# VectorE instead of TensorE turns u over from tile 6 on, and the state products join the scores-values step

## The chip, the core and the metric

The kernel runs on one core of a Trainium2 chip. The core has TensorE (matmuls, PE in the profile, with its weight loads as PEld), VectorE (DVE), ScalarE (ACT), GpSimd (POOL) and SyncE (SP, which issues every DMA of this kernel). Each engine works through its own queue in order; semaphores tie the queues together. TensorE writes only into PSUM, GpSimd here touches only SBUF. The metric is the device time of one execution in microseconds.

## What is computed

An attention layer with a recurrent state (batch 4, 8 heads, 768 steps, head size 40), then two dense layers on its 3072 tokens:

```
C = f_stab * C + i_stab * outer(v_t, k_t);  n = f_stab * n + i_stab * k_t
y_t = sigmoid(o_t) * (C q_t) / max(|n q_t|, 1)

h = x @ w_in                      # 320 -> 1024
solu = h * softmax(h)
ln = (solu - mean) / sqrt(var + 1e-6) * g_ln
x2 = ln @ w_out                   # 1024 -> 320

out = max(x2 @ w1, x2 @ w2, x2 @ w3) @ w_out2     # 320 -> 768 -> 320
```

## The kernel before

The recurrence is cut into chunks of 128 steps; a tile t is one chunk of one batch entry, 24 tiles (NT) in all, six (NC) to a batch entry. Within a chunk attention is a product of scores and values, and the state C passes from chunk to chunk. The 128 steps of a tile are also the 128 tokens that the dense layers take. Products in full precision are made of several matmuls on a high part (cast to fp32r) and the remainder; `split` (lines 299 to 303) makes both: a cast on ScalarE, then a subtraction on VectorE or GpSimd.

Each tile has several processes, generators that issue a few instructions and yield. The ORDER string, written out by a planner, is the order in which they are stepped, and so the order of every engine's queue and of the DMA queue: `A7*3` means three steps of process A of tile 7, and `~n` puts n dummy matmuls ahead. The processes that matter here:

- Q (`att_qk`, line 330) loads q and k; from tile 6 (NF) on it splits them into `qkh` and `qkl`, stores both to DRAM and loads them back stacked on 120 partitions. W makes the decay matrix, V loads values and weighted keys `kw`.
- S (`att_scores`, line 418) makes scores `ps` and multiplies them with the decay into `Pr`. I (`att_inter`, line 430) makes the part of the carried state, `pi`, from tile 6 on.
- Y (`att_out`, line 495) multiplies `Pr` with V into `py` (line 501), for tiles 1 to 5 adds C times q in the same PSUM group (line 504), adds `pi`'s part, and stores the result.
- T (`att_state`, line 457) makes the state products `pc` (line 472), adds them to the decayed C, and from C of tile 6 on splits it into `cst`, with two copies by DMA.
- X (`tokens`, line 530) loads the result with partitions as features, gates it and splits it into `xh` and `xl`.
- A (`layer1`, line 551): `ph` (two products into one PSUM tile with one buffer), its maximum (line 568), `e` = exp (line 571), `u` = ph * e (line 576), centred into `e` (line 580 on ScalarE or 582 on VectorE), squares summed (line 584), then `e` turned over in eight 128x128 blocks by TensorE into `pu` (line 592), four blocks to a PSUM tile, split in two halves into `uh` and `ul` (line 604), multiplied with w_out into `px` (line 613), scaled into `x2`, turned into `pq`, split into `x2h` and `x2l`. `e` and `u` have one buffer each; `ul` takes that of `e`, `uh` that of `u`.
- U (`layer2`, line 634) makes nine products `pe` per pair of tiles, in two PSUM buffers; P (line 652) takes the maximum of three and splits it into `h`; F (line 669) multiplies with the last weight into `po` and stores the output.

Three lists at the top say which of these operations run where: CENTER (the centring on ScalarE), POOL (the remainder of a split on GpSimd, and some products of X), VECTOR (the others on VectorE, GpSimd if not named; `P3` there is the remainder of `h`). PSUM tiles with tag "r" share four buffers.

## Time and profile before

| | us |
|---|---|
| median of 3 runs | 610.88 |
| lowest and highest | 607.91, 611.41 |
| the profiled execution | 608.91 |
| its span, first to last instruction | 607.1 |
| TensorE busy in it | 583.9 |
| VectorE busy | 380.0 |
| ScalarE busy | 345.0 |
| GpSimd busy | 198.6 |

Mean granted clock of TensorE: 0.975 of full speed. Busy times are of one profiled execution; matmuls overlap each other, so for what one costs TensorE the start of the next instruction is read, not the duration. "Idle before, releaser" in a row is the time that an engine waited and what ended it.

### The profile page before, as it was taken

Reading aid. Unit: us, or ns where it says so; the run is one execution under the profiler, and the core shown is the slowest. Engines: PE = TensorE matmul, PEld = TensorE weight load, DVE = VectorE, ACT = ScalarE, POOL = GpSimd, SP = SyncE. Lnnn points to the kernel's source line nnn. Section 1 sums busy time; section 2 is a strip of 40 time slices with the busy share of each in tenths; the row PEclk is TensorE's granted clock in tenths of the full one; section 3 lists DMA queues with packets and bytes.
Section 4 is the critical chain, followed back from the end, with each engine's and each line's share of the span. In section 5 each row is a group of like instructions: output and inputs, shape, how many; then the busy total and the mean of one; then the engine's idle time right before and its main releaser. Section 6 shows DMA issues by size and latency. Waiting matters only on the chain.

```text
span 607.1 us, 12327 instructions
## 1 busy us (share of the span) xinstructions
PE 583.9 (96%) x4688; PEld 542.7 (89%) x4688; DVE 380.0 (63%) x620; ACT 345.0 (57%) x671; POOL 198.6 (33%) x238
## 2 busy tenths in 40 slices
...
GB/s 301 335 201 269 262 203 213 259 230 179 162 148 169 159 64 118 231 217 206 156 107 183 185 180 204 195 173 181 144 207 219 85 40 19 37 5 11 12 32 25
DMA packets 56841, 95.97 MB, mean 158 GB/s; under 512 B 13926, under 2 KB 36510, under 8 KB 56782
## 3 DMA queue, kind: packets, MB, share of 16 engines
...
q14 instruction: 22, 0.18, 0.1%
...
## 4 chain that ended last, share of the span: by engine, by line
PE 74%; DVE 7%; DMA 7%; issue 4%; ACT 3%; SPq 2%; POOL 2%; DVEq 0%; ACTq 0%; POOLq 0%
PE pe L648 30%; PE px L613 12%; PE ph L566 11%; PE po L679 9%; PE pu L592 3%; PE py L501 3%; PE ps L423 3%; DMA nq<-rn 2%; PE pi L452 1%; PE pq L625 1%; POOL stA L269 1%; DMA qst<-qks 1%; PE pc L472 1%; DMA nd<-y 1%; DVE ul L302 1%
## 5 line engine op out<-in xcount | busy, mean ns | idle before, releaser
L648 PE MATMUL pe<-x2h,w 128*128 128x256 f32 x1080 | 166.8, 285 | 0.0
L648 PEld LDWEIGHTS pe<-x2h,w 128*128 128x128 f32 x1080 | 143.9, 189 | 2.0 <-issue 0.8
L648 PE MATMUL pe<-x2l,w 128*128 128x256 f32 x648 | 112.3, 282 | 0.0
L648 PEld LDWEIGHTS pe<-x2l,w 128*128 128x128 f32 x648 | 92.2, 188 | 0.0
L662 DVE TENSOR_TENSOR tmp<-pe,tmp 128x512 f32<-128x512 f32 x72 | 49.4, 686 | 55.9 <-PE pe L648 47.3
L679 PE MATMUL po<-w,h 128*128 128x320 f32 x432 | 67.6, 311 | 0.0
L566 PE MATMUL ph<-w,xh 128*128 128x512 f32 x240 | 65.9, 404 | 0.8 <-ACT xh L300 0.8
L613 PE MATMUL px<-w,uh 128*128 128x320 f32 x384 | 65.4, 313 | 0.4 <-DVE ul L302 0.4
L679 PEld LDWEIGHTS po<-w,h 128*128 128x128 f32 x432 | 63.7, 188 | 0.3 <-issue 0.2
L396 ACT ACTIVATE Wm<-Wm,aT 128x128 f32<-128x128 f32 x184 | 57.9, 393 | 6.4 <-POOL Wm L367 6.3
L613 PEld LDWEIGHTS px<-w,uh 128*128 128x128 f32 x384 | 58.8, 190 | 1.4 <-DVE ul L302 0.6
L566 PEld LDWEIGHTS ph<-w,xh 128*128 128x128 f32 x240 | 42.8, 191 | 8.5 <-ACT xh L300 1.1
L300 ACT CAST h<-tmp 128x512 fp32r<-128x512 f32 x36 | 22.2, 618 | 44.9 <-DVE tmp L662 44.9
L269 POOL TENSOR_TENSOR stA<-stA,raw 128x640 int32<-128x640 int32 x20 | 37.3, 1885 | 31.8 <-DVE raw L264 8.6
L367 POOL TENSOR_SCALAR_AFFINE_SELECT Wm<-Wm 128x1024 f32<-128x1024 f32 x24 | 28.9, 1205 | 54.3 <-DMA Wm<-rows_m 54.3
L576 DVE SCALAR_TENSOR_TENSOR u<-ph,e 128x1024 f32<-128x1024 f32 x24 | 29.2, 1216 | 26.0 <-ACT e L571 25.9
L426 DVE TENSOR_TENSOR Pr<-ps,Wm 128x512 f32<-128x512 f32 x48 | 32.2, 684 | 18.1 <-PE ps L423 11.2
L501 PE MATMUL py<-Pr,V 128*42 128x128 f32 x384 | 31.1, 290 | 12.8 <-DVE Pr L426 12.8
L571 ACT ACTIVATE e<-ph,st 128x1024 f32<-128x1024 f32 x24 | 26.8, 1117 | 25.8 <-PE px L613 18.9
L302 DVE TENSOR_TENSOR ul<-pu,uh 128x512 fp32r<-128x512 f32 x48 | 32.3, 685 | 14.3 <-ACT uh L300 7.8
L566 PE MATMUL ph<-w,xl 128*128 128x512 f32 x144 | 40.9, 392 | 0.0
L616 ACT ACTIVATE x<-px,st 128x320 f32<-128x320 f32 x24 | 12.6, 525 | 45.8 <-PE px L613 45.6
...
## 6 DMA issues: line engine op xcount, KB each, us to landing
...
```

Source lines behind the costliest of these rows:

```text
L269: pt(out=i32(A[:, j]), in0=i32(A[:, j]), in1=i32(low[:, j]), op=ALU.add)
L302: sub(out=lo, in0=x, in1=f(hi), op=ALU.subtract)
L367: nc.gpsimd.affine_select(out=W, in_=W, pattern=[[0, H], [1, P]], compare_op=ALU.is_ge, fill=-NEG, base=0, channel_multiplier=-1)
L396: nc.scalar.activation(out=W[:, h], in_=W[:, h], func=AF.Exp, scale=-1.0, bias=aT[:, c, b * H + h:b * H + h + 1])
L426: tt(out=Pr, in0=ps, in1=at[t, "W"][:, hh * 4:hh * 4 + 4], op=ALU.mult)
L501: mm(py[half(hh, VW), i], lhsT=at[t, "V"][:, hh * 4 + i], rhs=at[t, "P", hh][:, i], start=True, stop=(qg is None))
L566: mm(out_n, lhsT=a, rhs=x, start=(i == 0), stop=(i == len(passes) - 1))
L576: nc.vector.scalar_tensor_tensor(out=u, in0=ph, scalar=-2.0 ** -15, in1=e, op0=ALU.mult, op1=ALU.mult, accum_out=s(3))
L613: mm(px, lhsT=a, rhs=x, start=(i == 0), stop=(i == len(passes) - 1))
L648: mm(pe[:, j], lhsT=a, rhs=x, start=(i == 0), stop=(i == len(passes) - 1))
L662: tt(out=tmp, in0=pe, in1=tmp, op=ALU.max)
L679: mm(po[o], lhsT=h2[:, a, m, o * P:o * P + P], rhs=made[f"last{m // 2}"][:, x * WC + m % 2 * DM:][:, 0:DM], start=(m0 == 0 and i == 0), st ...
```

## The change

From tile 6 (NV) on, process A turns `e` over with VectorE: 16 instructions, each of eight 32x32 blocks (32 partitions x 256 elements), four to a step, from `e` into a new SBUF tile `eT`. The split of u is then one cast of 128x1024 and one subtraction of the same size, the latter on GpSimd for the tiles that POOL names with `u`. The transposes on TensorE and their PSUM tiles go for these tiles.

`state_products` is `pc`'s part of T as a function; from tile 6 (NJ) on, Y calls it right behind its own matmuls, in the same step. In Y all V products now come ahead of the products with C, and only the first matmul of a PSUM half starts it and only the last stops it. `qkl` is written over the raw tile. ORDER is the same up to the middle of its tenth line, but for one step of Q8 that comes later, and new from there, and the three lists are new: among others P0 to P9 leave VECTOR, all Q leave POOL. Of ORDER the lines around tiles 12 to 16 and 21 stand here.

```diff
--- before.py
+++ after.py
@@ -15,9 +15,9 @@
 AX = mybir.AxisListType
 ET = mybir.EngineType
 
-CENTER = "A0v A11v A14v A17v A18v A1v A21v A23v A2v A3v A4v A5v A6v A7v A8v"
-POOL = "D16 D19 Q10 Q11 Q19 Q20 Q21 Q22 Q23 Q7 X10s X12m X13s X14m X14s X16m X17m X18s X19s X1s X20m X20s X21m X21s X23m X23s X4m X4s X5m X5s X7m X7s X8m X8s"
-VECTOR = "I1 I2 I3 I4 I5 P0 P1 P11 P3 P4 P5 P7 P8 P9 T1 T10 T2 T3 T4 T7 V0 V1 V12 V13 V15 V18 V19 V2 V20 V4 V7 V9 X0g X11g X15g X17g X19g X21g X22g X23g X2g X3g X5g X6g"
+CENTER = "A0v A10v A11v A12v A13v A14v A15v A16v A19v A1v A20v A22v A23v A3v A4v A6v A8v A9v"
+POOL = "A11u A13u A14u A16u A21u A6u A7u D16 X0m X10m X10s X11s X13m X13s X14m X14s X16s X17s X20m X20s X21m X21s X22s X23m X2m X4m X4s X5m X6s X7m X7s X8s X9m X9s"
+VECTOR = "I1 I2 I3 I4 I5 P10 P11 T1 T10 T13 T16 T19 T22 V0 V1 V13 V15 V16 V18 V3 V4 V7 X0g X13g X14g X16g X17g X18g X1g X20g X3g X5g X6g"
 
 B, H, S, D = 4, 8, 768, 40
 P = 128
@@ -30,6 +30,8 @@
 K1 = FF1 // P
 K2 = FF2 // P
 NF = 6
+NV = 6
+NJ = 6
 NB = 1
 NA = 24
 VW = D + 2
...
+V16 X13 W15 A12 A11 A12 S15.0 X13*2 T14*2 T15 A11 I15 Q16 Q17 A12*2 Y14 P4 T14 S15.1 X13 U4 S15.0 U4 S15.1 Y14*2 P4
+A12 P4*3 W17 Y15 T15 U4 V16 A13 V18 W16 A12 P4 A12*2 W16 A11*2 A12 X14 Q17 I15*4 A12*3 A13 Y14 Q16 Q17 T15*2 P4*2 F4*3
+Y15 W17 U5*2 Y14 X14*2 S16.1 A12*2 T15*2 W16 S16.1 I16 S16.0*2 W18 X14 A12 A13*2 F4 X14*2 T16 A13 A12 P5 Y15 Q17 P5
+A13*2 I16 A14 W17 F4 I16*2 O5 A13*2 Q18 W17 Q18 F4 U5 P5 A14 A13 Y16 A13*2 U5 Y15 T16*2 Y15 Y16 Q17 P5 U5 P5 I16 V17
+P5 Y15 A13 Y16 A12 T16 Q18 P5 Y16 A14 U5 P5 Y16 A13*2 P5 O5 A14*2 U5 I17 P5 S17.1 S17.0 Q18 T16 P5 A13 S17.0 U5 A12
+S17.1 X15*3 T16 P5 A12 Y16 I17 X15 W18 A14 I17*2 U5 W18 X15*2 A13*2 P5 Y17 P5 Y17 Q19*3 P5 A15 Q18 X16*2 F3 A14 A13 F5
+I17 Y17 A14*2 Q19 F5 S18.0*2 A14*2 F5*2 X16 U6 Q20 A14*2 X16 P6 A15 V18 X16 Y17 X17 W19 V20 A14 S18.1 V20 W18 S18.1 U6
+A15 A14*2 Y17 Y18 A15 P6 Q19 T18 A14 U6 A15 W20 T18*2 X16 Q20 A15 U6 Y18 Y17 A16*2 Q20 T18 W19 T18 P6 F5 A15*2 S19.0
+A15*2 Y18 Q20 W19 P6 A14 A15*2 S19.0 A14 S19.1 A15*2 W19 S19.1 X17*2 I19*2 P6*2 X17 A16 U6 A15 Q21 U6 V19 Y18 I19*2
...
+A20*2 P8 U8 P8 U8 A18 A19 Y22 X21 S23.1 A20 P8*2 T22 W23 A20 X22 W23*3 A20*3 S23.0*2 A20 A21*2 A19*2 A20 U8 Y22 X22
+T22 A20 P8 X22 P8*2 A20*2 A21 A19 A21*2 P8 I23 F8 F5 U9 X22 F8*2 A20*2 I23 X22 S23.1 X22 F8 P9 A21*5 A20 A21 Y23 A21
+A22 A21*2 I23 Y23 A22 I23 U9*2 I23 Y23*3 A21 P9 X23 A21 A22 U9 A21*2 Y23 F7 P9*4 U9*2 X23 A21 X23*3 P9*4 A22*2 U9 P9
...
@@ -342,7 +343,7 @@
             dma(out=raw[64 * i:64 * i + 64], in_=src[t, :D].rearrange("d h p -> (d h p)").rearrange("(x y) -> x y", x=64))
         yield
         hi = att.tile([P, 5 * P], F32R, name="qkh")
-        lo = att.tile([P, 5 * P], F32R, name="qkl")
+        lo = raw.bitcast(F32R)
         yield from split(hi, lo, raw, on_pool(f"Q{t}"))
         for i, x in enumerate((hi, lo)):
             dma(out=qks[t, i].rearrange("a d h p -> (a d h p)").rearrange("(x y) -> x y", x=P), in_=f(x))
@@ -454,6 +455,15 @@
             tt(out=y[:, h4], in0=pi, in1=gb[:VW, h4], op=ALU.mult)
             yield
 
+    def state_products(t):
+
+        at[t, "pc"] = pc = psr.tile([P, 4, VW], F32, name="pc", tag="r")
+        warm(pc.rearrange("p a b -> p (a b)"))
+        for i in range(4):
+            for hh in range(2):
+                h = hh * 4 + i
+                mm(pc[half(hh, D), i], lhsT=at[t, "kw"][:, h], rhs=at[t, "V"][:, h], start=True, stop=True)
+
     def att_state(t):
 
         b, c = divmod(t, NC)
@@ -464,13 +474,10 @@
             on_vector(f"T{t}")(out=C, in0=Cs[t], in1=decb[:, b * H:(b + 1) * H, c:c + 1].to_broadcast([D, H, VW]), op=ALU.mult)
             yield
         Cs[t + 1] = C
-        pc = psr.tile([P, 4, VW], F32, name="pc", tag="r")
-        warm(pc.rearrange("p a b -> p (a b)"))
-        for i in range(4):
-            for hh in range(2):
-                h = hh * 4 + i
-                mm(pc[half(hh, D), i], lhsT=at[t, "kw"][:, h], rhs=at[t, "V"][:, h], start=True, stop=True)
-        yield
+        if t < NJ:
+            state_products(t)
+            yield
+        pc = at[t, "pc"]
         for hh in range(2):
             h4 = slice(hh * 4, hh * 4 + 4)
             if c:
@@ -498,10 +505,13 @@
         qg = at.get((t, "qg"))
         for i in range(4):
             for hh in range(2):
-                mm(py[half(hh, VW), i], lhsT=at[t, "V"][:, hh * 4 + i], rhs=at[t, "P", hh][:, i], start=True, stop=(qg is None))
-            for hh in range(2 if qg is not None else 0):
+                mm(py[half(hh, VW), i], lhsT=at[t, "V"][:, hh * 4 + i], rhs=at[t, "P", hh][:, i], start=(i == 0), stop=(i == 3 and qg is None))
+        for i in range(4 if qg is not None else 0):
+            for hh in range(2):
                 h = hh * 4 + i
-                mm(py[half(hh, VW), i], lhsT=cst[t][:, h], rhs=qg[:, h], start=False, stop=True)
+                mm(py[half(hh, VW), i], lhsT=cst[t][:, h], rhs=qg[:, h], start=False, stop=(i == 3))
+        if t >= NJ and (t + 1) % NC:
+            state_products(t)
         yield
         add = (t, "y") in at
         y = at[t, "y"] if add else att.tile([VW, H, P], F32, name="y", bufs=2)
@@ -584,14 +594,24 @@
         nc.scalar.activation(out=u, in_=u, func=AF.Square, scale=-1024.0, bias=s(3), accum_out=s(4))
         yield
         pus = []
-        for g in range(2):
-            pu = psr.tile([P, 4, P], F32, name="pu", tag="r")
-            warm(pu.rearrange("p a b -> p (a b)")[:, 0:256])
-            for i in range(4):
-                kk = g * 4 + i
-                nc.tensor.transpose(pu[:, i], e[:, kk * P:(kk + 1) * P], ident)
-            pus.append(pu)
-            yield
+        if t >= NV:
+
+            eT = moe.tile([P, K1, P], F32, name="eT")
+            e3 = e.rearrange("p (k n) -> p k n", n=P)
+            quarter = lambda i: slice(32 * i, 32 * i + 32)
+            for a in range(4):
+                for b in range(4):
+                    nc.vector.transpose(out=eT[quarter(b), :, quarter(a)], in_=e3[quarter(a), :, quarter(b)])
+                yield
+        else:
+            for g in range(2):
+                pu = psr.tile([P, 4, P], F32, name="pu", tag="r")
+                warm(pu.rearrange("p a b -> p (a b)")[:, 0:256])
+                for i in range(4):
+                    kk = g * 4 + i
+                    nc.tensor.transpose(pu[:, i], e[:, kk * P:(kk + 1) * P], ident)
+                pus.append(pu)
+                yield
         nc.gpsimd.tensor_scalar(out=s(5), in0=s(2), scalar1=1e-3, scalar2=1e-12, op0=ALU.mult, op1=ALU.add)
         pt(out=s(5), in0=s(5), in1=s(5), op=ALU.mult)
         pt(out=s(7), in0=s(4), in1=s(5), op=ALU.add)
@@ -599,6 +619,8 @@
         yield
         uh = moe.tile([P, K1, P], F32R, name="uh", tag="u")
         ul = moe.tile([P, K1, P], F32R, name="ul", tag="e")
+        if t >= NV:
+            yield from split(uh, ul, eT, on_pool(f"A{t}u"))
         for g, pu in enumerate(pus):
             sl = slice(g * 4, g * 4 + 4)
             yield from split(uh[:, sl], ul[:, sl], pu, tt)
```

## Rows read from the trace of the kernel before

**Rows 1.** The page, part 1: busy us (share of the span), instructions of each engine.

```profile
PE 583.9 (96%) x4688; PEld 542.7 (89%) x4688; DVE 380.0 (63%) x620; ACT 345.0 (57%) x671; POOL 198.6 (33%) x238
```

**Rows 2.** Windows: stretch, its us; PE, PEld, DVE, ACT, POOL busy; clock; DMA.

```profile
0.00:120.00 120.00, 101.77 (x793) 81.85 (x793) 110.91 (x164) 97.08 (x161) 62.41 (x52) 0.87 0.81 255
120.00:540.00 420.00, 418.13 (x3411) 397.93 (x3408) 250.86 (x430) 229.43 (x476) 128.56 (x174) 1.00 0.51 153
```

**Rows 3.** Waits of TensorE from 120 us on: total us, times, longest.

```profile
PE ps L423 <- DMA qks<-qkl: 1.2, 1, 1.2
PE px L613 <- DVE ul L302: 0.4, 1, 0.4
```

**Rows 4.** Timeline of TensorE (start, us, engine, line, operation): a group of pu.

```profile
565.25 0.60 PE L592 MATMUL pu<-ident,e 128*128 128x128 f32 x4
565.60 0.60 PE L648 MATMUL pe<-x2h,w 128*128 128x256 f32 x3
```

**Rows 5.** Timeline of TensorE: py of tile 3; py, pc, pu of a later tile.

```profile
75.41 0.42 PE L501 MATMUL py<-Pr,V 128*42 128x128 f32 x4
...
78.20 0.55 PE L625 MATMUL pq<-ident,x 128*128 128x128 f32 x3
...
324.80 1.08 PE L501 MATMUL py<-Pr,V 128*42 128x128 f32 x16
325.70 0.48 PE L472 MATMUL pc<-V,kw 128*40 128x42 f32 x16
326.11 0.66 PE L592 MATMUL pu<-ident,e 128*128 128x128 f32 x4
326.52 0.73 PE L648 MATMUL pe<-x2h,w 128*128 128x256 f32 x4
```

**Rows 6.** Lines by form: busy us, mean ns of one, then idle before.

```profile
L568 DVE TENSOR_REDUCE st<-ph 128x1 f32<-128x1024 f32 x24 | 29.2, 1217 | 6.0 <-PE ph L566 5.8
L580 ACT ACTIVATE e<-u,st 128x1024 f32<-128x1024 f32 x15 | 17.3, 1151 | 5.0 <-DVE u L576 5.0
L302 DVE TENSOR_TENSOR ul<-pu,uh 128x512 fp32r<-128x512 f32 x48 | 32.3, 685 | 14.3 <-ACT uh L300 7.8 <-PE pu L592 6.2
L300 ACT CAST w<-stA 128x1024 fp32r<-128x1024 f32 x6 | 6.3, 1049 | 2.9 <-DVE dec L204 2.8
L302 POOL TENSOR_TENSOR w<-stA,w 128x1280 fp32r<-128x1280 f32 x1 | 3.0, 2953 | 0.0
L479 DVE COPY C<-pc 40x168 f32<-40x168 f32 x8 | 2.6, 327 | 0.2
```

**Rows 7.** Timeline of VectorE: one undisturbed, a pair on two halves, two overlapping.

```profile
306.65 0.56 DVE L544 TENSOR_TENSOR xr<-xr,nq 128x384 f32<-128x384 f32 x1 [4.62 <-POOL Cl L490]
...
309.38 1.38 DVE L511 TENSOR_TENSOR y<-py,y 42x512 f32<-42x512 f32 x2
...
322.36 0.67 DVE L426 TENSOR_TENSOR Pr<-ps,Wm 128x512 f32<-128x512 f32 x1
322.95 0.67 DVE L662 TENSOR_TENSOR tmp<-pe,tmp 128x512 f32<-128x512 f32 x1
```

**Rows 8.** The chain that ended last, in order of time: start us, us, what.

```profile
299.11 1.92 PE pe L648 x16
...
313.69 0.40 PE ps L423 x4
314.09 0.35 PE pq L625 x3
...
320.41 0.24 PE pi L452 x4
320.65 1.88 PE ph L566 x8
...
571.98 3.52 PE px L613 x24
575.50 2.64 PE po L679 x18
```

More of the change, by code (lines that the diff above doesn't have):

```diff
@@ L51 @@
 A0*5 A1*2 Llast1 A0*3 D13 Q4 Y2 V6 D13*2 T3 W4 Y2 V3 D11 A1 Y3 D11 A0*2 Q6 Q7 W5 Q7 A1 Q7 Y3 X2 A0*2 Y2 S4.1*2 A1 Y3
[L52 removed]
+A1 T3*2 I4 W5 S4.0 A1*4 D11 X2 Llast0 D13 X2 A1 I4 X2 V4 A1*3 S4.0 Y3 D11 D15 W5 D13 A1 Q5 T4 X2 W6*2 X2 Q7 Q8 D13*2
 Y4 A1*2 A2~2 I5 Y4 D15 V4 A1 U0 T4 X3 D13 Y4 Q8 S5.1 O1 D15 V5 D13 P0 W5 D15 S5.0 D17*2 U0 Y3*2 I5 O1 D17 S5.1 D17 A2
[L54 removed]
@@ L95 @@
-F10*2 U11 P11 U11 P11 U11~5 P11*2 U11 P11*2 U11 P11 U11 P11 F10*2 P11 F7 P11 U11*2 P11 U11 F11*2 P11*4 F11*6
+Y4 T4 Q6 S5.0 X3 U0 W6 D17 A2*2 D17 Y5*2 Llast2 P0*3 Y5 D15 A2 X4 X3 U0 Lm2_2 S6.1 Q8 D15 Q8 U0 W11 X3*2 A2*2 D17 A2*2
+W6 X3 D15*2 Y4 A2*2 S6.0 Y4 A3 S6.1 A3 A2*4 V7 P0 S6.0 D15 Y5*2 D16*2 X4 P0 D16 Q9 U0 D19*2 P0 A2 A3 X4 D16 X4*2 A3 V6
+Y6 X4 A3 D16 U0 A4 W7 A3*2 W7 X5 Q7 P0 Y5 A3*2 T6 D16 A4 I7 T6*2 X5 A3 A2 Q9 D19*2 A3*3 W7 A3*2 T6*2 A2*2 S7.1 V7
+D16*2 X5*2 Q9 I7 P0 D16 Q9 A4 P0 Y6*2 W11 S7.0 V10 T7 P0 U0 W7 A4 S7.0 A3 S7.1 O2 A4 X5 I7*3 P0 A4 Y7 A4 T7 Q10 A3 X5
@@ new lines @@
+U0 P0 W8 O2 D19 A4*2 I8 Y7 A5 Y6 Q8 Y7 Q10 A4 Q10 A4*2 Q10 W8 A5 T7 A4*2 A3 D19 W8 A5 P0 T7 X6 P0 V8 D19 T7 A4 Q11 T7
+A3 U1 Y7 W8 S8.1*2 F0*2 V8 F0 Y6*2 S8.0 T8 S8.0 W9 Y7 W9 A5*2 F0*3 I8 P1 U1 P1 X6*2 I8*2 U1 Y8 X6 A4*2 A5 Q9 W9 T8 I8
+T9 T8 X6 A5 U1 X6 P1*2 Y7 U1 A5*2 Y8 P1 X7 P1 X7 Y8 X7 A5*2 S9.1 A6*2 A5 V9 T8 I9 T8*2 P1 S9.0 W9 S9.1 Y8 Q11 X8 X7*2
+A6 U1 V10 A4 A5 W11 Y8 A5*2 U1 S9.0 V9 Y9 A6*2 A5 Y8 X8*2 X7 W10 P1*3 A4 T9 A5*3 U1 I9 Q11 I9*2 P1 A6 Q10 U1 T9 W10
+A6*2 T9*2 P1 A7 P1 X8 I9 Q11 P1 U2 A6 W10 P1 F1*2 S10.1 Y9 S10.0 Q12 Y9*2 F1*2 I10 W11 A6*2 Y9 A6*3 V11 Q12*2 T9 P2 A7
```

62 lines of the change are left out of this document (20 added, 42 removed).

## The prediction

> **What bounds the kernel now.** I read the page's busy times first. TensorE is busy for 96% of the span and VectorE for 63% [rows 1]; a share over the whole span mixes stages, so the windows come next. From 0 to 120 us TensorE is idle for 18 us, its granted clock averages 0.87, and VectorE is busy 111 of 120 us. From 120 to 540 us TensorE is busy 418 of 420 us at full clock while VectorE is busy 251, 60% [rows 2]. The waits of TensorE after 120 us say the same: 1.2 us for a DMA, 0.4 us for a `ul` [rows 3]. So from 120 us on, time comes off only by taking work off TensorE, and what is put on VectorE costs nothing as long as TensorE does not begin to wait for it. Before 120 us VectorE is the fuller engine; there the change leaves the turn of tiles 0 to 5 on TensorE.
>
> **The change, part by part.**
>
> *The turning of u leaves TensorE.* Eight transposes per tile go, in 18 tiles (6 to 23). Matmul durations overlap, so I take start to start: a group of four holds TensorE from 565.25 to 565.60, 0.35 us [rows 4]; behind products of another shape from 326.11 to 326.52, 0.41 us [rows 5]. Thirty-six groups are 12.6 to 14.8 us; I take 13.4, nearer to the first, since most groups stand like it. TensorE had no idle time there, so this is a gain one for one unless something is late.
>
> *V products before state products in tiles 1 to 5.* Before, they alternate in groups of four: tile 3's 32 take 75.41 to 78.20, 2.79 us. Unmixed, 16 V products take 0.90 us (324.80 to 325.70) [rows 5]. The trace has no unmixed run of the 40-row products; between nothing saved and the V products' rate for both (2 x 0.90 = 1.80, 1.0 saved) I take 0.7. Only tiles 3 to 5 lie where TensorE is full, so 2.1 us (0 to 3).
>
> *State products (`pc`) join the step of `py` from tile 6 on.* In the rows `pc` already stands right behind `py`, 0.41 us (325.70 to 326.11) [rows 5]. I cost the move itself at 0: the matmuls stay on TensorE, and the DMAs of `cst` behind them are as many. What it can cost is a later C: SyncE's queue carries the two `cst` copies, and behind those whatever DMA comes next. The cover is the next tile's `pi` standing several steps further on; if it is gone, `pi` (0.24 us) waits for a `cst` copy, and TensorE with it.
>
> *Edits that I cost at nothing.* `qkl` is written over `qkr`, so the next tile's load of q and k waits for this tile's store; the cover is that the load stands a tile or more ahead of its `ps`. If that is gone, `ps` waits, as it did once for 1.2 us [rows 3]. `eT` has one buffer, but its next writer follows its last reader on the same engine or behind a whole tile's work. The start and stop marks of `py` leave its matmuls as many.
>
> *VectorE gets 16 transposes per tile*, each 32 partitions x 256 elements. The trace has no VectorE transpose. Nearest rows: a copy of 168 elements takes 0.327 us, an SBUF operation of 384 elements 0.56 when undisturbed; on the line between them 256 elements take 0.42 [rows 6, 7]. Lower bound: successive operations on the same partitions overlap (0.67 us long, the next 0.59 after the start), the overlap is 0.08, so 0.34. But two that move to another partition half do not (the pair of `y` takes 1.38 for two of 0.69) [rows 7], and every transpose here writes another quarter than the one before: I take 0.42. Upper bound: each element costs twice, 0.42 + 256 x 1.06 ns (the slope of that line) = 0.69. At 0.42 a tile's turn takes 6.7 us of VectorE in place of 0.75 us of TensorE.
>
> The Trainium skill, "VectorE: DVE Perf Modes", section "The three transpose paths", gives 311 ns for a 128-element turn in bf16. An estimate from it with this slope is 0.45 us; the sum below would then end about 5 us higher. Its section "Rules for kernel authors" advises TensorE for a full 128x128 turn if PSUM will do as the destination, which speaks against this change; by it the gain above would not come.
>
> *The rest of VectorE's load.* Added: 18 x 6.7 = 121 us, and 8 `qkl` that were GpSimd's (8 x 0.83 for 640 elements on the line above, 6.6). Removed: 36 half `ul` of 0.685 (24.7), of which 11 whole ones of 1.22 come back (13.4); 21 `h` remainders of the same size as a half `ul`, now on GpSimd (14.4); some 5 us of `e` and `kw`, estimated by their sizes. Net about +97 us, nearly all after 120 us: 251 becomes some 348 of 407, 85% [rows 2, 6]. GpSimd's price by its one row of this kind is 2.3 ns an element (2.953 us for 1280): it gains 21 `h` of 1.2 and 7 `ul` of 2.4 and loses 8 `qkl` of 1.5, with some `kw` added: some +35 us on 199 [rows 1]. Neither is full.
>
> *Is TensorE made to wait?* The chain from a tile's second `ph` to its `px` gets longer: `max` 1.22, `exp` and then `e` on ScalarE 1.15 each, `u` and `ul` on VectorE 1.22 each like the maximum of that size, turn 6.7, `uh` in one cast 1.05 [rows 6], with other work of the new ORDER between. I laid TensorE's steps (`pe` 1.92, `px` 3.52, `po` 2.64, `ph` 1.88, `ps` 0.40, `pq` 0.35, `pi` 0.24 [rows 8], `py` 0.90 and `pc` 0.41 [rows 5]) beside VectorE's for three tiles, both in the order written, from the end of the second `ph`:
> - Tile 15: TensorE reaches `px` after ps, pe, px14, py+pc, pq, 2 pe, 2 ph, 2 ps, pi, pe = 18.1 us. VectorE holds `u` back behind the sum of C, which needs the `pc` done at 7.2; `u` ends at 9.0, `e` at 10.2, a max at 10.4, the turn at 17.1, `Pr` and `x2l` at 18.2, `ul` at 19.4. Late by 1.3.
> - Tile 12: 5 pe, 2 ph, po, py+pc, 4 ps, 2 pi, pq = 19.7 us; turn from 8.1 with 1.6 us of other work inside ends at 16.5, four small operations follow, `ul` ends at 20.0. Late by 0.3.
> - Tile 21: 4 pe, px20, 2 po, 2 ph, py, 2 pi, 2 pq = 22.3 us; the turn ends at 15.6, `ul` on GpSimd (2.4) at 19.0. In time by 3.3.
>
> The mean lateness is 0.53 us; 18 tiles would lose 9.6. A stalled TensorE gives VectorE a start on the next tile, so I take 7.
>
> **Sum**, against the profiled execution's own 608.9 us (span 607.1 and 1.8 around it): 608.9 - 13.4 - 2.1 + 7 = 600.4, said as 600.5. The runs shown have a median of 610.9 (607.9 to 611.4), 2.0 above; I leave the forecast on the profiled scale.
>
> **Rivals.**
> 1. *No lateness*: the transposes overlap after all (0.34 us; the turn is 1.3 us shorter, which clears tiles 12 and 15). 608.9 - 15.5 = 593.4. For it: the 0.08 overlap of ordinary operations; against: the `y` pair.
> 2. *VectorE gives the gain back*: at 85% an engine that works in order is late more often than in my three tiles, by 0.63 to 1.3 us a tile: 605 to 617. For it: a sub in every tile now follows the whole turn instead of half of it. Against: some 60 us of VectorE idle remain. The Trainium skill's advice above would land here.
> 3. *Slower: a transpose costs by bytes.* This one thing decides: each 0.01 us on it adds 0.16 us to the chain of tiles 12 and 15, some 1.9 us in all with tile 21's slack. From 0.49 us on lateness reaches 1.31 us a tile and the time 617; at 0.69 the three tiles are 5.6, 4.6 and 1.0 late, 3.7 in the mean, 18 x 3.7 = 67, 660 us. For it: no 4-byte transpose in the trace; against: every other 4-byte row goes by elements.
> 4. *C is late instead*: `pc` behind `py` makes `pi` wait for `cst`, up to a few us in 15 tiles. Part of rival 2's sum, not beside it.
>
> **How the numbers follow.** Likeliest case 0.36 (its own range 596 to 605), rival 1 0.22 (592 to 596), rival 2 with 4 0.24 (605 to 617), rival 3 0.18 (617 to 660). A measurement of this kernel tells about 1%, 6 us, from no change: the first two cases are faster, 0.58; rival 2 is the same, 0.24; rival 3 is slower, 0.18. For 8 in 10 the range goes from 592 to 618 and leaves out most of rival 3.
>
> **What would show it.** The transposes' row: 288 of them, 0.42 us each, start to start as long. TensorE busy down by some 15 us, `pu` at 48 matmuls; waits of `px` for `ul` of some 7 us where there were 0.4; tile 3's `py` step near 2.1 us; VectorE near 85% between 120 and 530 us. I am wrong if the transposes are over 0.49 us, if TensorE waits for another releaser (`cst`, `Pr`, `xh`), or if TensorE's own steps grow.

## The result and the profile after

The changed kernel takes 617.38 us (median of 4 runs, 614.34 to 619.43), the kernel before beside it 609.46: a ratio of 1.0117 with a 95% interval of 1.0072 to 1.0162. It is slower by just over 1% where 1.4% faster was forecast. The profiled execution takes 617.43 us, its span 615.6.

The page, part 1, of the kernel after; it answers to [rows 1]:

```profile
PE 576.6 (94%) x4544; PEld 536.9 (87%) x4544; DVE 485.5 (79%) x862; ACT 348.2 (57%) x656; POOL 229.1 (37%) x263
```

TensorE was relieved of only 7.3 us, while the span grew by 8.5: it now stands idle for 39.0 us of the span where it was 23.2. VectorE got 105 us more (97 were forecast). Where TensorE's idle time lies is in the windows, beside [rows 2]:

```profile
0.00:120.00 120.00, 97.09 (x736) 82.93 (x737) 107.32 (x152) 91.42 (x156) 58.49 (x53) 0.83 0.79 248
120.00:540.00 420.00, 408.31 (x3271) 384.64 (x3270) 341.71 (x648) 233.23 (x461) 162.65 (x199) 1.00 0.52 155
```

From 120 to 540 us TensorE is idle for 11.7 us where it was 1.9, with VectorE at 81% where it was 60%. The waits of TensorE in that stretch, the answer to [rows 3] (total us, times, longest):

```profile
PE px L635 <- POOL ul L303: 2.7, 4, 1.2
PE px L635 <- DVE x2l L303: 1.9, 1, 1.9
PE px L635 <- DVE ul L303: 1.7, 2, 1.0
PE pq L647 <- DVE y L455: 1.0, 1, 1.0
PE pe L670 <- DVE tmp L684: 0.7, 1, 0.7
PE px L635 <- DVE y L521: 0.7, 2, 0.5
PE pe L670 <- DVE x2l L303: 0.7, 1, 0.7
PE py L508 <- DVE Pr L427: 0.6, 1, 0.6
...
PE px L635 <- ACT uh L301: 0.3, 1, 0.3
```

Only 4.7 us of it are waits for a tile's own `uh` and `ul`. Nearly all of the rest (6.5 of 6.9 us, the rows left out counted) is other work of VectorE (`x2l`, `y`, `tmp`, `Pr`) that comes late.

What the new operations cost, lines by form of the kernel after (busy us, mean ns of one, idle before):

```profile
L604 DVE STREAM_TRANSPOSE eT<-e 32x256 f32<-32x256 f32 x288 | 125.4, 435 | 5.0 <-ACT e L590 0.7
L303 DVE TENSOR_TENSOR ul<-eT,uh 128x1024 fp32r<-128x1024 f32 x11 | 13.4, 1218 | 2.7 <-ACT uh L301 2.7
L303 POOL TENSOR_TENSOR ul<-eT,uh 128x1024 fp32r<-128x1024 f32 x7 | 17.6, 2511 | 27.2 <-ACT uh L301 27.0
L301 ACT CAST uh<-eT 128x1024 fp32r<-128x1024 f32 x18 | 18.9, 1048 | 41.3 <-DVE eT L604 41.2
```

**The loss by stage.** A cut that both kernels share is the first product `px<-w,uh` of a tile. Up to that of tile 7 both have done the same matmuls, but for the 16 transposes `pu` of tiles 6 and 7 and the V products of one `py` and one `pi`, which the new order places otherwise; between tile 7's and tile 23's they differ by these and by 16 tiles of `pu`. Tile 7's starts at 219.2 us before and 226.8 after: 7.6 us later. Windows from there to tile 23's (571.8 before, 580.25 after; here and below a window is cut within 0.3 us of these starts), first of the kernel before, then of the kernel after (columns as in [rows 2]):

```profile
219.20:571.80 352.60, 350.79 (x2838) 334.53 (x2837) 194.87 (x338) 176.25 (x365) 87.82 (x131) 1.00 0.45 134
```

```profile
226.70:580.00 353.30, 342.08 (x2694) 322.91 (x2695) 289.24 (x557) 183.92 (x356) 117.29 (x149) 1.00 0.44 133
```

This stretch, where the whole gain was to come, lasts as long as before (353.3 for 352.6). From tile 23's `px` to the end it is 35.3 and 35.4. So there are two questions: what eats the gain of 16 tiles, and what costs 7.6 us before tile 7.

### The profile page after: what moved, and what is told of

Read it like the earlier page. It is cut to its first block, busy times and chain, and to the rows that moved or that the text cites. A ratio compares the mean times of both kernels' runs of the same rounds, so it can differ in the third digit from the quotient of the medians.

```text
span 615.6 us, 12274 instructions
## 1 busy us (share of the span) xinstructions
PE 576.6 (94%) x4544; PEld 536.9 (87%) x4544; DVE 485.5 (79%) x862; ACT 348.2 (57%) x656; POOL 229.1 (37%) x263
## 4 chain that ended last, share of the span: by engine, by line
PE 34%; DVE 28%; DMA 18%; ACT 7%; issue 7%; SPq 3%; POOL 2%; DVEq 0%; ACTq 0%; POOLq 0%
PE pe L670 15%; DVE eT L604 14%; PE px L635 8%; PE po L701 4%; PE ph L576 3%; DMA qkr<-kt 3%; DMA qks<-qkr 3%; DMA q<-qt 2%; DMA nq<-rn 2%; DVE tmp L684 2%; DMA nd<-y 2%; DMA qst<-qks 2%; PE py L508 2%; ACT uh L301 2%; POOL ul L303 2%
## 5 line engine op out<-in xcount | busy, mean ns | idle before, releaser
L604 DVE STREAM_TRANSPOSE eT<-e 32x256 f32<-32x256 f32 x288 | 125.4, 435 | 5.0 <-ACT e L590 0.7
L303 POOL TENSOR_TENSOR h<-tmp,h 128x512 fp32r<-128x512 f32 x30 | 38.9, 1297 | 117.2 <-ACT h L301 112.0
L635 PE MATMUL px<-w,uh 128*128 128x320 f32 x384 | 67.0, 318 | 3.5 <-DVE x2l L303 1.9
L270 POOL TENSOR_TENSOR stA<-stA,raw 128x640 int32<-128x640 int32 x20 | 35.6, 1799 | 35.2 <-DVE raw L265 27.2
L301 ACT CAST uh<-eT 128x1024 fp32r<-128x1024 f32 x18 | 18.9, 1048 | 41.3 <-DVE eT L604 41.2
L635 PE MATMUL px<-w,ul 128*128 128x320 f32 x192 | 37.6, 318 | 4.4 <-POOL ul L303 2.7
L508 PE MATMUL py<-Pr,V 128*42 128x128 f32 x384 | 28.5, 289 | 13.8 <-DVE Pr L427 13.8
```

Source lines behind the costliest of these rows:

```text
L270: pt(out=i32(A[:, j]), in0=i32(A[:, j]), in1=i32(low[:, j]), op=ALU.add)
L301: nc.scalar.copy(out=hi, in_=x)
L303: sub(out=lo, in0=x, in1=f(hi), op=ALU.subtract)
L508: mm(py[half(hh, VW), i], lhsT=at[t, "V"][:, hh * 4 + i], rhs=at[t, "P", hh][:, i], start=(i == 0), stop=(i == 3 and qg is None))
L604: nc.vector.transpose(out=eT[quarter(b), :, quarter(a)], in_=e3[quarter(a), :, quarter(b)])
L635: mm(px, lhsT=a, rhs=x, start=(i == 0), stop=(i == len(passes) - 1))
```

## Experiments

Each time is a median, each ratio against the kernel before on the same chip, with its 95% interval.

### How long the turn takes

`quick_turn` shortens VectorE's part to price it: it leaves out the move of the blocks between the quarters of the partitions, so `u` is not turned as a whole.

```diff
-                for b in range(4):
-                    nc.vector.transpose(out=eT[quarter(b), :, quarter(a)], in_=e3[quarter(a), :, quarter(b)])
+                nc.vector.transpose(out=eT[:, :, quarter(a)], in_=e3[:, :, quarter(a)])
```

> The kernel after, with the 16 VectorE transposes of a tile replaced by 4, each over all 128 partitions and 256 elements. It leaves out the move of the 32x32 blocks between the quarters of the partitions, so that u is not turned as a whole; TensorE, ScalarE, GpSimd and the written order stay as they are, VectorE is spared about 12 x 0.435 = 5.2 us in each of 18 tiles. Theory 1, VectorE's 7 us of turn make the steps of TensorE behind them late: TensorE's idle time between 120 and 540 us falls from 11.7 to about 2 us, the waits of px for ul and uh fall below 1 us together, the time is 606 to 609 us (ratio 0.995 to 1.0). Theory 2, it is the new written order and the other new waits (tmp, x2l, y, the loads of q and k) that cost, whatever the turn takes: the idle time stays at 9 us or more and the time at 614 to 618 (ratio 1.008 to 1.015).

596.29 us, 0.9788 (0.9752 to 0.9824): faster by more than theory 1 foresaw. The kernel gets 21 us back when 12 of a tile's 16 transposes go, and TensorE's idle time from 120 to 540 us falls to 1.4. `turn_10` has that edit in two of a tile's four steps alone, so the turn takes 4.3 us:

> The kernel after, with 10 transposes per tile from tile 6 on: two of the four steps with 4 of 32 partitions each, the other two with one of 128 partitions each (u is not turned as a whole). The turn takes 8 x 0.435 + 2 x 0.416 = 4.3 us, VectorE about 437 us. With 4 transposes the time was 596.3, with 16 it was 617.4. If the loss is in proportion: 605 to 608 us (ratio 0.993 to 0.998). If it grows from a point on (queueing): 597 to 602 us (ratio 0.98 to 0.988). If the first microseconds cost most: 610 to 616.

600.03 us, 0.9816 (0.9767 to 0.9865). The loss is not in proportion. The windows from tile 7's `px` to tile 23's, of turn_10 and then of quick_turn:

```profile
226.70:561.80 335.10, 335.10 (x2698) 320.75 (x2698) 244.73 (x461) 180.98 (x352) 113.55 (x148) 1.00 0.45 139
```

```profile
222.80:558.60 335.80, 335.41 (x2698) 320.81 (x2698) 201.75 (x365) 180.87 (x351) 116.12 (x148) 1.00 0.46 138
```

TensorE is idle for 0.0 and 0.4 us in all, and the stretch takes 335 us. A turn of 4.3 us costs nothing there; the whole turn costs 18.2 us (353.3 less 335.1). The 3.7 us between the two kernels' times arise before tile 6, where they are the same program: tile 7's `px` starts at 226.7 in one profile and 222.8 in the other. That is also how far one profile of the first stage can be trusted.

How the turn makes others late is seen at tile 15, in the timeline of VectorE of the kernel after (start us, us from the first start to the last end, operation):

```profile
395.23 2.05 DVE L303 TENSOR_TENSOR qkr<-qkr,qkh 128x640 fp32r<-128x640 f32 x1
397.20 0.68 DVE L684 TENSOR_TENSOR tmp<-pe,tmp 128x512 f32<-128x512 f32 x1
397.80 7.17 DVE L604 STREAM_TRANSPOSE eT<-e 32x256 f32<-32x256 f32 x16
405.00 0.69 DVE L427 TENSOR_TENSOR Pr<-ps,Wm 128x512 f32<-128x512 f32 x1
405.61 0.55 DVE L303 TENSOR_TENSOR x2l<-pq,x2h 128x384 fp32r<-128x384 f32 x1
406.14 1.23 DVE L303 TENSOR_TENSOR ul<-eT,uh 128x1024 fp32r<-128x1024 f32 x1
```

and of TensorE, from the second `ph` of tile 15 on:

```profile
383.76 0.86 PE L576 MATMUL ph<-w,xl 128*128 128x512 f32 x3
...
386.81 1.34 PE L635 MATMUL px<-w,uh 128*128 128x320 f32 x8
389.40 0.85 PE L635 MATMUL px<-w,ul 128*128 128x320 f32 x4 [1.25 <-POOL ul L303]
390.09 1.33 PE L635 MATMUL px<-w,uh 128*128 128x320 f32 x8
...
403.76 0.51 PE L670 MATMUL pe<-x2l,w 128*128 128x256 f32 x3
406.16 2.22 PE L635 MATMUL px<-w,uh 128*128 128x320 f32 x8 [1.89 <-DVE x2l L303]
...
411.32 0.76 PE L670 MATMUL pe<-x2h,w 128*128 128x256 f32 x5
```

VectorE takes its work in the order written. Sixteen transposes stand ahead of `Pr` and of `x2l`, the remainder of another tile, and it has no idle time from 395.2 on; `px` waits 1.89 us for that `x2l`, not for its `ul`. `px` does not read `x2l`. It takes over the PSUM buffer of tile 14's `pq`: of the four that tag "r" shares, `ps`, `ps` and `pi` took the other three in between, and `x2l` reads `pq` last (405.61 and 0.55 us on, 406.16, `px` starts). So a late reader on VectorE holds up a product that has nothing to do with its tile. Behind this wait the granted clock of TensorE, 1.00 before, fell to 0.50, its lower level of 1.2 GHz, until 410.0:

```profile
406.60:409.90 3.30, 3.30 (x14) 3.30 (x14) 3.27 (x5) 1.16 (x4) 0.00 (x0) 0.50 0.21 78
```

In turn_10 the same work follows without a gap too, first of VectorE, then of TensorE:

```profile
388.13 0.68 DVE L686 TENSOR_TENSOR tmp<-pe,tmp 128x512 f32<-128x512 f32 x1
388.73 1.77 DVE L606 STREAM_TRANSPOSE eT<-e 32x256 f32<-32x256 f32 x4
...
392.77 0.45 DVE L604 STREAM_TRANSPOSE eT<-e 128x256 f32<-128x256 f32 x1
393.14 0.65 DVE L427 TENSOR_TENSOR Pr<-ps,Wm 128x512 f32<-128x512 f32 x1
393.71 0.54 DVE L303 TENSOR_TENSOR x2l<-pq,x2h 128x384 fp32r<-128x384 f32 x1
```

```profile
395.05 1.33 PE L637 MATMUL px<-w,uh 128*128 128x320 f32 x8
396.21 0.75 PE L637 MATMUL px<-w,ul 128*128 128x320 f32 x4
396.80 1.34 PE L637 MATMUL px<-w,uh 128*128 128x320 f32 x8
...
398.56 0.76 PE L672 MATMUL pe<-x2h,w 128*128 128x256 f32 x5
```

From the turn's start to that of `x2l` it is 5.0 us there and 7.8 after. The 2.8 us are the difference between no wait of TensorE and one of 1.89 us.

Both kernels give TensorE the same matmuls in the same order, so its start-to-start times can be laid side by side. At tile 15 the 24 matmuls of `px` take 5.16 us to the next product (406.16 to 411.32) where turn_10 takes 3.51 (395.05 to 398.56): the lower clock costs 1.65 us. At tile 14 the steps from 386.81 to 390.09 take 3.28 us where turn_10's from 395.05 to 396.80 take 1.75: a wait of 1.25 us costs 1.53, 0.18 of it up to the first matmul behind the wait and 0.10 in the four that follow. Added up so over some twenty places of the stretch, the waits for a tile's own `uh` and `ul` cost about 7.5 of the 18.2 us, those for other work, nearly all VectorE's, with the lower clock about 10.3; 0.4 us are spread.

### VectorE's total, or the place of the work

Two kernels keep VectorE about as busy and differ in where. `load_later` is quick_turn with 12 transposes of an unused tile behind `px`, `x2` and `pq`:

```diff
+        for b in range(4 if t >= NV else 0):
+            nc.vector.transpose(out=idle[32 * b:32 * b + 32], in_=idle[32 * (b ^ 1):32 * (b ^ 1) + 32])
```

> The kernel with 4 transposes of 128 partitions per tile (u is not turned as a whole), and 12 further transposes of 32x256 per tile on an unused tile, in three groups of 4 behind the steps px, x2 and pq of the same tile, so that VectorE works as long as in the kernel after (about 486 us) but not ahead of px. If it is the occupancy of VectorE that costs, the idle time of TensorE between 120 and 540 us is 8 us or more and the time 610 to 617 us (ratio 1.0 to 1.015). If it is the duration of the turn ahead of the tile's own px, the idle time stays below 4 us and the time is 596 to 600 (ratio 0.979 to 0.987).

641.75 us, 1.0532 (1.0491 to 1.0574), worse than the turn itself and above both ranges. From tile 7 to tile 23:

```profile
226.80:606.50 379.70, 351.32 (x2698) 330.21 (x2698) 289.78 (x561) 181.05 (x351) 114.55 (x147) 0.97 0.41 122
```

VectorE's busy time in the stretch is that of the kernel after (289.8 and 289.2 us), and TensorE is idle for 28.4 us where it was 11.2; part of the rest of the loss is its granted clock, 0.97 for 1.00. So the duration ahead of the tile's own `px` is not needed for the loss: the same time of VectorE at places that the order has not planned for costs more. The other way round, `lighter_dve` keeps the whole turn and lifts other work off VectorE; it is built on `own_lo` (below), which gives `qkl` its own tile and takes 612.97 us:

```diff
-VECTOR = "... P10 P11 T1 T10 T13 T16 T19 T22 V0 V1 V13 V15 V16 V18 V3 V4 V7 X0g X13g X14g X16g X17g X18g X1g X20g X3g X5g X6g"
+VECTOR = "... P10 P11 T1 V0 V1 V3 V4 X0g X1g X3g X5g"
+POOL = "... D16 Q10 ... Q23 Q7 Q8 Q9 X0m ..."
```

> The kernel after with qkl in its own tile and the whole turn of 16 transposes, and 35 small operations moved from VectorE to GpSimd by the lists: the rests of q and k of tiles 7 to 23 (17 x 1.06 us), the gates' products of 7 tiles (0.58), 5 products kw (0.64) and 6 products of C (0.71). VectorE falls by about 18 + 4 + 3 + 4 = 29 us to 456, GpSimd rises by about 17 x 1.6 + 7 x 1.07 + 5 x 0.81 + 6 x 0.77 = 43 us to 272 (45%). With qkl's own tile alone it is 613. If VectorE's total counts, on the line between 437 us (600) and 485 us (617), less 3 for the tile: 600 to 606 us (ratio 0.985 to 0.994). If the bursts of 1.74 us on VectorE ahead of others' work count whatever the total, or GpSimd becomes late: 611 to 620.

618.10 us, 1.0129 (1.0080 to 1.0178). My expectation fell. VectorE is busy for 467.8 us instead of own_lo's 485.4 (17.6 less where I had counted 29), yet:

```profile
227.30:580.60 353.30, 341.50 (x2696) 321.54 (x2697) 277.44 (x532) 184.01 (x357) 145.40 (x174) 1.00 0.44 133
```

The stretch takes 353.3 us, as in the kernel after, and 352.2 in own_lo. Less work in total brought nothing, but it is a weak test: of VectorE's 289 us in the stretch only 12 are gone, where turn_10 takes off 45. Whether some of this kernel's waits come from GpSimd, 38 us busier, can't be told apart; from 120 to 540 us its `xl` made TensorE wait for 1.1 us and `cst` copies for 1.7, waits that the kernel after does not show.

### The turn without its order, the order without its turn

`turn_only` is the kernel before with its own order and lists, the turn on VectorE from tile 6 on, and `qkl` over `qkr` (with the nine loads moved as below):

```diff
+        if t >= NV:
+            eT = moe.tile([P, K1, P], F32, name="eT")
...
+        if t >= NV:
+            yield from split(uh, ul, eT, tt)
```

> The kernel before with u turned over by VectorE from tile 6 on, in the ORDER and with the lists of before; all u remainders on VectorE. qkl is written over the raw tile, as the new tile eT needs the room, and nine loads of Q stand later in ORDER for that. Lateness theory: TensorE's work falls by 13.4 us, but VectorE gets 288 x 0.435 = 125 us without any relief and an ORDER that did not reckon with it; TensorE's waits for ul after 120 us come to 15 us or more, time 610 to 630. Rival, the new ORDER and lists are at fault and the turn is good in itself: 597 to 603.

723.48 us, 1.1874 (1.1837 to 1.1911); against raw_alone below (635.40), the same kernel without the turn, 88 us more, and far above both ranges. TensorE's waits over the whole span show it:

```profile
PE px L631 <- ACT uh L306: 64.6, 15, 9.0
```

`px` waits up to 9 us for `uh`, in 15 places. `turn_back_17` is the kernel after with the turn on TensorE again in all tiles but 19:

```diff
-        if t >= NV:
+        if t in (19,):
```

> The changed kernel with u turned over by TensorE again in 17 of the 18 tiles (only tile 19 stays on VectorE); its ORDER, its lists, the joined state products and the rest stay. Lateness theory (the turn makes VectorE late, and TensorE's 9.8 us of new idle time after 120 us come from that): TensorE's work rises by 17 x 0.75 = 12.7 us and the idle time of 11.7 us between 120 and 540 us falls to about 2, so the time stays within 4 us of the changed kernel's 617. Rival, the rest of the new ORDER and the queues cost it: the idle time stays near 10 us and the time goes to about 630.

634.85 us, 1.0402 (1.0360 to 1.0445). That is near the rival's 630 and not the 617 that I expected: TensorE, with its work of 17 turns back, still stands idle for 15.2 us from 120 to 540 us. I read the two together so: the written order of the change and the turn on VectorE belong together, and either without the other is slower than both kernels. So turning single tiles back could not serve to size the turn; shortening it could.

### The first tiles

**qkl over qkr.** `own_lo` gives `qkl` a tile of its own again, and `eT` the two buffers of `stA` for room; `et_two_bufs` has the second edit alone.

```diff
-        lo = raw.bitcast(F32R)
+        lo = att.tile([P, 5 * P], F32R, name="qkl")
...
-            eT = moe.tile([P, K1, P], F32, name="eT")
+            eT = moe.tile([P, K1, P], F32, name="eT", tag="stA", bufs=2)
```

> The changed kernel with qkl in a tile of its own again; for the room, eT takes the two buffers of the weight decoding, free by then. Queue theory (SyncE's queue stands still for 28 us in ten places because the load of the next q and k waits for the store out of the same tile, and the other transfers queued behind it come late): those waits go, TensorE's idle time falls by some 5 us in the first 120 us and by 5 or more of 9.8 later, 603 to 609. Rival, the rest of the new ORDER or lateness of VectorE is what costs: 614 or more.

> The control to the run before it: the changed kernel with eT in the two buffers of the weight decoding, qkl still over the raw tile. Both theories: within 2 us of the changed kernel's 617, since one eT was hardly waited for.

612.97 us, 1.0068 (1.0046 to 1.0091) and 616.16 us, 1.0119 (1.0093 to 1.0146): the shared tile costs 3.2 us. The waits of SyncE's queue in the kernel after show how:

```profile
SPq L343 <- DMA qks<-qkr: 28.3, 10, 5.2
```

The load of the next q and k (L343) stands in the queue until the store out of the same tile has landed, ten times, and every later DMA stands behind it. Before, this row was not there. Done in the kernel before it shows at full size: `q_order` moves the nine loads that stood ahead of the store right behind it (the cut shows one, its order's repeats written short), `raw_alone` writes `qkl` over `qkr` as well.

```diff
-D15 Q8 W5 D13 A1 Q5 T4 X2 W6*2 X2 Q7 D13*2
+D15 W5 D13 A1 Q5 T4 X2 W6*2 X2 Q7 Q8 D13*2
...
-        lo = att.tile([P, 5 * P], F32R, name="qkl")
+        lo = raw.bitcast(F32R)
```

> The kernel before with the nine loads of Q later in ORDER, each right behind the store of the tile before, but qkl in its own tile: the control to raw_alone, which differs only in the shared tile. Queue theory: the load waits for nothing there, so 609 to 614, and the 25 us that raw_alone lost come from the waiting load at the head of the queue. Rival, the late places of the loads cost it: 625 or more.

> The kernel before with qkl written over the raw tile, nine loads of Q later in ORDER, nothing else. Theory that SyncE's queue is what costs the first 120 us (the load of the next q and k stands in the queue behind a store, 28 us of such waits in the changed kernel): 613 to 616, with TensorE idle in the first 120 us up from 18 to about 23 us. Rival, the lists cost it there: within 2 us of before.

615.50 us, 1.0099 (1.0069 to 1.0129) and 635.40 us, 1.0415 (1.0362 to 1.0468): 20 us for one shared buffer when load and store are next to each other, far more than the 4 to 7 us that I expected of it. In the change's own ORDER the load comes 1 to 42 steps behind the store, and 3.2 us are left.

**The products of py.** `py_regroup` is the kernel before with the V products of tiles 1 to 5 ahead of the state products:

```diff
-                mm(py[...], lhsT=V..., start=True, stop=(qg is None))
-            for hh in range(2 if qg is not None else 0):
+                mm(py[...], lhsT=V..., start=(i == 0), stop=(i == 3 and qg is None))
+        for i in range(4 if qg is not None else 0):
+            for hh in range(2):
```

> The kernel before with the V products of tiles 1 to 5 ahead of the state products, nothing else. By the step of the forecast: tile 3's step takes 2.0 us for 2.8 and the time falls by 2 (0 to 3). Rival, the first 120 us wait for something else: no change.

612.35 us, 1.0051 (1.0029 to 1.0073). The step itself got as short as forecast, in the timeline of TensorE of the kernel after (tile 3, beside [rows 5]):

```profile
79.55 1.07 PE L508 MATMUL py<-Pr,V 128*42 128x128 f32 x16
80.56 1.07 PE L512 MATMUL py<-gb,C 40*42 40x128 f32 x16
81.56 0.55 PE L647 MATMUL pq<-ident,x 128*128 128x128 f32 x3
```

79.55 to 81.56 is 2.01 us, where it was 2.79. But nothing follows earlier for it: in py_regroup TensorE's busy time of the first 120 us is 99.8 instead of 101.8, all of it turned into idle time, and tile 7's `px` starts at 219.3 us (219.2 before).

**The lists.** `lists_early` puts the entries of tiles 0 to 5 back as before; `early_back` does so, gives `qkl` its own tile and interleaves `py` in tiles 0 to 5 again.

```diff
-POOL = "... X0m X10m ... X2m X4m X4s X5m X6s ..."
+POOL = "... D19 X10m ... X1s ... X4m X4s X5m X5s X6s ..."
-VECTOR = "I1 I2 I3 I4 I5 P10 P11 T1 ... X1g ..."
+VECTOR = "I1 I2 I3 I4 I5 P0 P1 P10 P11 T1 ... T2 T22 T3 T4 ... X2g ..."
```

> The changed kernel with the entries of the three lists for tiles 0 to 5, P0 to P2 and D as before. If the new lists cost the first 120 us (X1's remainder moved to VectorE, which TensorE then waits 1.5 us for, and the clock falls to half again at 79 to 86 and 97 to 100 us): 611 to 613, TensorE idle in 0 to 120 us back to about 18 us. If SyncE's queue does: no difference.

> The kernel after with its first six tiles put back: the entries of the three lists for tiles 0 to 5 and pairs 0 to 2 as before, the V and state products of tiles 0 to 5 interleaved as before, and qkl in a tile of its own (eT takes the two buffers of stA for room). The turn on VectorE from tile 6 on and its written order stay. Theory 1, the loss of the first 120 us (TensorE busy there 97.1 us where it was 101.8) comes from these three together: the first 120 us show TensorE busy 101 to 102 us at a clock of 0.87 again, and the time is 607 to 609.5 (ratio 0.996 to 1.0). Theory 2, the loss is not in them (each alone gave little: lists +2.5 us against after, products nothing, own qkl tile -3.2): 0 to 120 us stays below 99 us and the time is that with qkl's own tile, 612 to 614 (ratio 1.005 to 1.009).

620.38 us, 1.0190 (1.0158 to 1.0222), and 614.32 us, 1.0086 (1.0058 to 1.0113). The lists put back alone gained nothing, so they were not what cost the first stage. (The falls of the clock that I had put at 79 to 86 and 97 to 100 us lie at 69 to 75 and 86 to 89 us of the span, at 0.50 in both; I had read them from another zero.) The first 120 us of early_back are as theory 1 wanted them, TensorE busy and clock alike:

```profile
0.00:120.00 120.00, 102.63 (x764) 82.81 (x765) 110.12 (x162) 96.41 (x161) 58.26 (x50) 0.87 0.82 257
```

The time is not: tile 4's `px` is 4.7 us earlier than after (145.8 and 150.4), tile 7's only 1.9 (224.9 and 226.8). `early_quick`, both edits in one, ends where quick_turn did:

> The two edits above in one kernel: the first six tiles as before with qkl in its own tile, and 4 VectorE transposes for the 16 of a tile, so that u is not turned as a whole. If lateness by the turn and the first 120 us are the two causes and independent, the time is before less the TensorE time saved in 18 tiles: 609.5 - 13 = 596 to 600 us (ratio 0.978 to 0.985), with less than 4 us of TensorE idle between 120 and 540 us. If a third cause remains (the written order itself), it is 603 to 609.

595.41 us, 0.9764 (0.9727 to 0.9801). The early edits are worth 1 us there, within what two such kernels differ by. From tile 4's `px` to tile 7's it is 79.2 us in early_back, 76.0 in early_quick and 74.7 in the kernel before. So early_back loses most of what it had gained again behind tile 4, where the new ORDER begins and tiles 6 and 7 are turned, and a good part of that is the length of these two turns.

### Another engine for the burst

If VectorE turns 128 partitions at a time, the blocks must change quarters elsewhere. `act_moves` lets ScalarE do it while it writes `e`, `act_moves_half` in every other tile; `pool_moves` and `pool_moves_half` use GpSimd (with `qkl` in its own tile).

```diff
+        def move(a):
+            for b in range(4):
+                nc.scalar.activation(out=e3[quarter(b), :, quarter(a)], in_=u3[quarter(a), :, quarter(b)],
+                                     func=AF.Identity, scale=-1024.0, bias=s(3)[quarter(a)])
...
+                    nc.vector.transpose(out=eT[:, :, quarter(a)], in_=e3[:, :, quarter(a)])
```

> The kernel after, with the turn done in full but in another way from tile 6 on: ScalarE writes e from u in 16 pieces of 32 partitions x 256 elements, each to the quarter of the partitions that it belongs to after the turn (estimate 0.35 us each, from 1.15 us for 1024 elements and 0.62 for 512: 5.6 us a tile where one pass took 1.15), and VectorE turns the 32x32 blocks with 4 instructions of 128 partitions (0.416 each). From u to the end of the turn it is 5.6 + 1.7 = 7.3 us where it was 1.15 + 7.0 = 8.1. VectorE falls from 485 to about 385 us, ScalarE rises from 348 to about 430. If VectorE's occupancy cost the 21 us and ScalarE at 72% does not take its place: 597 to 603 us (ratio 0.98 to 0.99). If the duration between e and px costs, or ScalarE becomes the late one: 610 to 618 (ratio 1.0 to 1.015).

> As before it, in the even tiles from 6 on alone (9 of 18): VectorE about 435 us, ScalarE about 390. If occupancy counts and more than in proportion (queueing), it is below the middle between the kernel after and the one with ScalarE in all tiles, perhaps the best of the three: 600 to 606 us (ratio 0.985 to 0.995). If the duration counts: 610 to 618.

698.34 us, 1.1473 (1.1438 to 1.1508), and 657.01 us, 1.0812 (1.0769 to 1.0855).

> The kernel after with qkl in its own tile, and from tile 6 on e written from u by GpSimd in 16 pieces of 32 partitions x 256 elements, each to its quarter, so that 4 VectorE transposes of 128 partitions end the turn; the whole turn is done. From the rows of GpSimd (1.16 us for a pass with one input over 1024 elements, 0.23 us for a tiny one) a piece is estimated at 0.45 us (0.3 to 0.7), a tile at 7 us (5 to 11), GpSimd at 228 + 130 = 360 us, VectorE at 388, ScalarE at 330. If GpSimd has room for the burst: 598 to 606 us (ratio 0.982 to 0.995). If its ul, xl, h and C steps come late behind the burst, as ScalarE's did: over 620 (ratio over 1.02).

> As before it, in the even tiles from 6 on alone (9 of 18): GpSimd about 295 us, VectorE about 435. If GpSimd has room: between the kernel with all tiles and that with qkl in its own tile (613), 600 to 609 us (ratio 0.985 to 1.0). If not: 615 to 640.

718.30 us, 1.1787 (1.1742 to 1.1831), and 669.25 us, 1.0985 (1.0941 to 1.1029). The pieces, lines by form of act_moves and of pool_moves:

```profile
L596 ACT ACTIVATE e<-u,st 32x256 f32<-32x256 f32 x288 | 145.6, 506 | 15.1 <-DVE u L586 11.2
```

```profile
L596 POOL TENSOR_SCALAR e<-u,st 32x256 f32<-32x256 f32 x288 | 141.3, 491 | 80.9 <-DVE u L586 57.7 <-PE pe L686 0.7
```

A piece costs 0.51 us on ScalarE where I had estimated 0.35 from long rows, so a tile takes 8.1 us. GpSimd's was as estimated (0.49 for 0.45), and that kernel is the slowest of the four: GpSimd is busy 374 of 715 us, about half. What TensorE then waits for is the other work of the engine that got the burst: in act_moves 11.9 us for ScalarE's `tmp` and 10.2 for its `x`; in pool_moves 13.3 for GpSimd's `xl`, 7.6 for its `kw`, and 14.1 for `tmp` of ScalarE, which stands waiting for `e` itself (120 to 540 us). All four are 51 us or more above the ranges that I had given them for a good outcome: the burst does to the new engine's other work what it did to VectorE's. No kernel run here that computes everything was faster than the kernel before.

## Why the prediction was wrong

Where the sum went: it took 8.5 us off, and the span grew by 8.5. Of the growth 7.6 us arise before tile 7's `px`. In the stretch to tile 23's some 17.5 us were gained and 18.2 lost again.

**Read rightly.** The bound after 120 us: with VectorE out of the way (turn_10) TensorE is busy for 335.1 of 335.1 us. The price of a transpose: 0.435 us for the 0.42 taken, and start to start as long, 12 in 5.39 us, 0.45 each. So a tile's turn is 7.2 us for 6.7, and rival 3 (from 0.49 on) was not met. `ul` 1.22 and 2.51 (1.22 and 2.4 taken), `uh` 1.05, VectorE's share 81% (85%), tile 3's `py` step 2.01 (2.1), `pu` at 48 matmuls.

**The gain, -13.4: right in kind, if anything small.** The stretch from tile 7 to tile 23 falls from 352.6 to 335.1 in turn_10. Of the 17.5 us, 0.9 are the 16 V products that the order moved ahead of the cut (less 0.24 for four `pi` that it moved behind), and 1.8 idle time that is gone; some 15 us are left for 16 tiles. The start-to-start reading of [rows 4, 5] gave 0.74 a tile, 11.9 for these; added up over all 128 transposes of the stretch in the trace of before it is 12.4. What the other 2.6 us are stays open. The Trainium skill ("VectorE: DVE Perf Modes", section "Rules for kernel authors") advises TensorE for a full 128x128 turn that may land in PSUM; in this kernel's sum the runs agree (617.4 us for 609.5), although the price of the transposes alone did not decide it.

**The failed step is the lateness, +7: it was 18.2 us in the 16 tiles.** The prediction asked one question of three tiles: when is `ul` ready for the tile's own `px`? That part was sized well: these waits came to 4.7 us from 120 to 540 us, and to about 7.5 us of the stretch with what follows each of them. It did not ask who else stands behind the turn on VectorE. The other waits from 120 to 540 us are `x2l`, `y`, `tmp` and `Pr`. Tile 15 shows one of them: the last reader of a PSUM buffer that the next product takes over. By the kernel's text those of `px` and `pq` for `y` and of `pe` for `tmp` are of the same kind, since no product reads `y` or `tmp`; I did not follow each. With the lower clock that followed the longest of them they cost some 10.3 us, which the sum had at nothing. My own sign of being wrong, "if TensorE waits for another releaser", is what came. I had even laid out tile 15 with `Pr` and `x2l` behind the turn, and took the time of `ul` alone. The layout also began with free engines. In the trace the turn of tile 15 begins 13.2 us behind the second `ph` (384.6 to 397.8) and not 10.4, because `u` ends 1.7 us later than laid out and a remainder of q and k of 2.05 us stands between; TensorE, held by tile 14's `ul`, reaches `px` 1.6 us later than laid out, so only a part of that is hidden.

Of the 18.2 us, 11.2 are idle time of TensorE; 7.0 are busy time with the same matmuls, of which 1.65 is the lower clock at tile 15 and most of the rest what each wait costs beyond its idle time.

Rival 2 came nearest ("an engine that works in order is late more often than in my three tiles"), with 605 to 617 us and a chance of 0.24; the time lies just past its upper end. But its reason was `ul`, which follows the whole turn, and not the other readers. Its point "some 60 us of VectorE idle remain" is true and no help, since the idle time is not where the turn is. That the range of 592 to 618 holds the time is owed to rival 2; the forecast inside it, a faster kernel, did not come. That the length of the turn makes the loss is shown by quick_turn and turn_10; that the place of VectorE's work counts and not its total alone, by load_later, and lighter_dve agrees weakly. How much room each place has was not measured.

**The -2.1 of the V products: the step got shorter, the kernel did not.** The sentence that failed is "tiles 3 to 5 lie where TensorE is full". My own [rows 2] had TensorE idle for 18 us of the first 120 with VectorE busy for 111.

**The 0 for `qkl` over `qkr`: 3.2 us.** The cover that I named was the distance from the load to its `ps`. TensorE's `ps` indeed hardly waited; the load held SyncE's queue instead, and what was queued behind it. I had named that way of costing for `cst` and not for this edit.

**The state products in the step of `py`: 0, as forecast**, as far as it can be seen: `pi` waited for `cst` hardly at all in the kernel after.

**What stays open.** Up to tile 7's `px` the kernel after loses 7.6 us. The shared tile is 3.2 of the loss, by times; early_back recovers the busy time and the clock of the first 120 us, yet little of the total. Five kernels that are the same program up to tile 4's `px` (after, et_two_bufs, quick_turn, turn_10, load_later) reach it at 147.3 to 151.8 us, all later than the kernel before and py_regroup (144.5 and 144.6). So there is a loss, but the rest, some 4 us, is no larger than this scatter. The new ORDER from its tenth line on was not taken back by itself in any run.
